# Attention and a gated layer on one core: output weights beside the gated values, maxima moved by ScalarE, earlier token sums, other ranks

## The chip, the cores and the metric

The kernel runs on one core of a Trainium2 chip. The core has TensorE (PE in the profile, with its weight loads as PEld), VectorE (DVE), ScalarE (ACT), GpSimd (POOL) and SyncE (SP); SP issues every transfer of this kernel. The metric is the device time of one execution in microseconds.

## The reference

Linear attention over 8 batches of 8 heads with 576 tokens and 64 columns, and a gated layer on its output, all in float32:

```python
def phi(x):
    proj = np.einsum('bhsd,df->bhsf', x, w_phi)
    proj = proj - np.max(np.abs(proj), axis=-1, keepdims=True)
    return np.concatenate([np.exp(proj), np.exp(-proj)], axis=-1)
q_p, k_p = (phi(q), phi(k))
kv = np.einsum('bhsf,bhsd->bhfd', k_p, v)
z = np.sum(k_p, axis=2)
num = np.einsum('bhsf,bhfd->bhsd', q_p, kv)
den = np.einsum('bhsf,bhf->bhs', q_p, z)[..., None] + 1e-06
x = (num / den).transpose(0, 2, 1, 3).reshape(4608, 512)
gate = 1.0 / (1.0 + np.exp(-(x @ w_gate)))      # w_gate: 512 x 1536
return (gate * (x @ w_val) @ w_out)             # w_out: 1536 x 512
```

## The kernel before

**Arithmetic.** Every large product is made of three: each operand is split into a high part, rounded to the float32r format, and a low part, the rest, and high x high, high x low and low x high are summed in PSUM. So each weight and each activation lies in SBUF twice (`wh`/`wl`, `xh`/`xl`, `hh`/`hl`).

**Stages.** The 1536 hidden columns are twelve blocks `j` of 128.
- *Attention*: 32 pairs of heads (`attend(i)`, four to a batch). For each, PE projects K token by token (L431, tails L447/L451) and Q feature by feature (L536; the first three pairs, `on_pe`, do Q another way, L497 to L518). DVE takes K's maxima (L437) and subtracts them (L466), ACT makes the two exponentials (L478). Then PE multiplies with V (L620) and sums K's features over the tokens (L634), turns the result (L646), and forms the numerators (L662) and denominators (L680).
- *First blocks*: blocks 0 to 3 for nine chunks `c` of 512 tokens (`gate`, L913, and `mm_out`, L970), woven between the pairs. A chunk needs all the pairs of its tokens; chunks 7 and 8 need the last batch. Results go to DRAM (`yscr`).
- *Passes*: blocks 4 to 11, four at a time (`pass_over`, two halves of six stretches of 768 tokens). There the gate and value products are done with seven instead of eight block products (`group`, L1228) from combined weights (`combine`), and the output products are L1310. One stretch is 168 matmuls of L1228 and 72 of L1310.

**Q's maxima** (pairs from the fourth on). DVE takes maxima within squares of 32 by 32 (L558) into `pm`, 128 partitions by 36. `across` (L567 to L576), one operation of the plan on DVE, takes the maximum over all 128 partitions: two copies of 64 partitions and four of 32 into `pn`, and two maxima. Then come the transposition to `mb` (L579) and the subtraction (L586).

**Token sums.** For pairs `i < ONPE` PE does the sums over K's tokens in five steps of four matmuls, four with `ones` as weights and one with `halves`: 20 in the source, 40 in the profile, where each of these float32 matmuls stands twice. For `i >= ONPE` DVE adds four blocks of tokens first (L599, L606, into `su`), and L634 has two steps, 16 matmuls in the profile.

**SBUF.** `low` (86 KiB a partition) and `flat` last through the kernel. Attention's buffers lie at the other end, and are replaced at `swap()`, once all attention work is done, by `high` (72 KiB) and `more`. In `low`, in the first part: `r_wh`, `r_wl` 0 to 32 KiB, `r_xh`, `r_xl` to 48, `r_oh`, `r_ol` to 64, `r_hh`, `r_hl` to 84. For the passes the same memory is cut anew: `r_X` (the tokens) 0 to 42 KiB, `r_y1` to 48, `r_h` (the gated values) to 72, `r_stage` to 86. `high` holds `r_G`, the combined weights, 0 to 56 KiB and `r_wo`, the output weights of four blocks, to 72; for chunk 7 its tokens `r_x7` lie at 42 to 58 KiB. In L1310 the gated values are the stationary operand and `wo` the moving one; in L1228 the weights from `high` are stationary and the tokens from `low` moving; in L913 and L970 weights `wh`/`wl` and gated values `hh`/`hl` are stationary, tokens and output weights `r_oh`/`r_ol` moving.

**Output weights.** For the first half, `out_weight` computes the weights of blocks 4 to 7 straight into `r_wo`. Those of blocks 8 to 11 are computed during the first stretches into `r_stage`, stored to DRAM (`kept`, `wscr`) and fetched into `r_wo` for the second half (`fetched`).

**Order.** `Plan` is a list scheduler that runs when the kernel is built. Each operation has an engine, an estimated time, its buffers and a rank; of the operations of an engine that could start at about the same time, the lowest rank goes first, and on PE a change of kind adds `STICK` to the rank. The result is a fixed order of instructions on each engine and of transfers in SP's queue. Ranks: pair `i` has `due(i) = START + PERIOD * (i - 4)` from the fifth pair on, its kv step `KOFF` later, its numerators `NOFF` later. A chunk has `due` of the pair after its last one, plus `LEAD`; its block `j` has `2 * j * FSTEP` more, its outputs `(8 + t) * FSTEP`. Weight `m` of block `j` has `(3 * j + m) * WSTEP`. The passes begin at rank `due(32) + 60 + 150`.

Of the kernel before, what the change touches and what calls it, by code (L numbers as in the profile page):

```python
# [20 lines left out]
P = 128  # L21
# [16 lines left out]
CELL = 64  # L38
RA = 86 << 10
RB = 72 << 10  # L40
FB = 15 << 10
NQ = 3
LATE = 7
ONPE = 12
BANKS = 5
PERIOD = 16.4
START = 56.0
LEAD = 90.0
STICK = 6.0
WAT = 0.0  # L50
WSTEP = 6.0
RAW = 6
XN = 4
HN = 5
FSTEP = 4.5
KOFF = 20.0
NOFF = 40.0
HSTEP = 2.0
# [209 lines left out]
def attention_moe(  # L268
# [87 lines left out]
    r_h = x.ring(8, 2 * HT)  # L356
    r_stage = x.ring(2, 7 * 2 * P)
    x = high()
    r_G = x.ring(8, 7 * 2 * P)
    r_wo = x.ring(8, DM)  # L360
    r_x7 = high(42).ring(2 * NC4, CW)
# [45 lines left out]
    def attend(i):  # L407
# [121 lines left out]
        else:  # L529
# [23 lines left out]
            )  # L553
            pm, pn = at("pm", 2, [P, nj]), at("pn", 2, [P, nj])
            mb = at("mb", 1, [P, 2, S])
# [10 lines left out]

            def across():  # L567
                vec.tensor_copy(pn()[0:64], pm()[64:128])
                vec.tensor_copy(pn()[64:128], pm()[0:64])
                vec.tensor_tensor(pm(), pm(), pn(), op=ALU.max)  # L570
                for a in range(4):
                    o = a ^ 1
                    vec.tensor_copy(pn()[a * 32 : a * 32 + 32], pm()[o * 32 : o * 32 + 32])
                vec.tensor_tensor(pm(), pm(), pn(), op=ALU.max)

            plan.op("DVE", 1.6, 0.16, across, [], [pm, pn], r + 7)  # L576
            dve(
# [751 lines left out]
    for n in range(2):  # L1329
        r = base - 30.0 + 30.0 * n  # L1330
        for m in range(2):
            ws[n, m] = combine(n, m, r + 10.0 * m, [r_G], [])
        for j in pair(n):
            wo[j] = out_weight(j, r + 20.0, [r_wo], [])
    start = base + 150.0
    for dc in range(NDC):
        r = start + SPAN * dc
        pass_over(
            (0, 1), dc, r, ws, wo, yscr, ymark, lambda c, t: y2scr[c][t], y2mark
        )  # L1340
        if dc < 4:
            n, m = 2 + dc // 2, dc % 2
            mark = marks[n, m] = Buf()
            kept(combine(n, m, r + KEEP, [r_stage], [done]), gscr[n, m], mark, r + KEEP)
            j = JA + 4 + dc
            mark = marks[j] = Buf()
            kept(out_weight(j, r + KEEP + 10.0, [r_stage], [done]), wscr[j], mark, r + KEEP)

# [68 lines left out]
```

## Time and profile before

| | us |
|---|---|
| median of three runs | 1168.27 |
| lowest, highest | 1164.08, 1170.7 |
| the profiled execution's own time | 1167.91 |
| its span, first to last instruction | 1166.0 |
| last matmul of attention (L680) ends | 516.4 |
| first product of the passes (L1228) | 598.7 |
| one stretch of a pass (L1228, L1310) | 29.13 + 16.79 |
| DVE, ACT busy | 933.6, 583.3 |

How to read it: a line such as `L1310 PE MATMUL gate<-high,low` names the source line, the engine, the operation, the tile that is written and the arenas that are read; `128x512` is partitions by columns. Where a helper records operations, the line is that of the helper. Matmuls are pipelined: the time of one is the distance of the starts, not the length of its bar, so a row of the chain divided by its count gives it.

### The profile page before, as it was taken

To read this page: it belongs to the slowest core of one execution; us is meant where nothing else is said; L and a number is where in the kernel's file an instruction comes from. 1 tells how busy PE (TensorE), PEld (TensorE's weight loads), DVE (VectorE), ACT (ScalarE), POOL (GpSimd) and SP (SyncE) were. 2 spreads that over 40 slices of the span, in tenths; PEclk is the share of its full clock that TensorE was granted. 3 is DMA by queue.
4 is the path that set the end of the run, shared out by engine and by line. 5 is a ranking of instruction groups with operands and counts; after the bars stand their busy time and mean duration, and the time that the engine had idled before them with its cause. 6 is when DMAs were issued, how large, how long until landed. Compare 5 with 4: busy or idle time off the path is not lost.

```text
span 1166.0 us, 22301 instructions
## 1 busy us (share of the span) xinstructions
PE 1148.7 (99%) x8796; PEld 939.5 (81%) x8796; DVE 933.6 (80%) x1793; ACT 583.3 (50%) x1115; POOL 0.7 (0%) x6
## 2 busy tenths in 40 slices
PE   8999999999999999999999999999999999999998
PEld 6666566776676777778879899899899898998997
DVE  6999989888878878848987999998766756857764
ACT  6767776666657666626553444352332332423421
POOL 0000000000000000000000000000000000000000
PEclk9999999999999999999999999999999999999999
DMA  7674553444425353225334646645557424224232
GB/s 235 202 242 126 151 169 120 133 125 126 146 80 160 108 155 103 79 79 193 116 99 152 204 142 238 181 147 179 163 178 278 143 93 122 81 89 157 59 91 82
DMA packets 97136, 166.88 MB, mean 143 GB/s; under 512 B 18568, under 2 KB 43272, under 8 KB 97032
## 3 DMA queue, kind: packets, MB, share of 16 engines
q1 hardware_dynamic: 97032, 165.46, 44.8%
q8 instruction: 69, 1.13, 0.4%
q14 instruction: 35, 0.29, 0.1%
HBM read 117.96 MB, written 47.32 MB: 142 GB/s over the span
## 4 chain that ended last, share of the span: by engine, by line
PE 85%; DVE 8%; DMA 5%; ACT 1%; issue 1%; SPq 0%; DVEq 0%; ACTq 0%
PE bank L1228 30%; PE gate L1310 17%; PE gate L913 11%; PE gate L970 7%; PE bank L620 4%; PE bank L662 3%; PE bank L431 2%; DMA rb<-den 2%; PE bank L680 2%; PE bank L913 2%; PE bank L536 1%; DMA den<-dn 1%; PE bank L970 1%; DVE d L586 1%; PE bank L634 1%; PE bank L646 1%
## 5 line engine op out<-in xcount | busy, mean ns | idle before, releaser
L1228 PE MATMUL bank<-low,high 128*128 128x384 f32 x2016 | 352.3, 336 | 0.9 <-DVE low L1190 0.7
L1228 PEld LDWEIGHTS bank<-low,high 128*128 128x128 f32 x2016 | 349.8, 188 | 2.7 <-DVE low L1190 1.0
L1310 PE MATMUL gate<-high,low 128*128 128x512 f32 x864 | 203.6, 395 | 0.0
L1310 PEld LDWEIGHTS gate<-high,low 128*128 128x128 f32 x864 | 162.3, 188 | 37.9
L913 PE MATMUL gate<-low 128*128 128x512 f32 x708 | 168.4, 394 | 1.2 <-ACT flat L948 0.6
L913 PEld LDWEIGHTS gate<-low 128*128 128x128 f32 x708 | 130.8, 188 | 30.2 <-issue 1.2
L478 ACT ACTIVATE ek<-ek 128x512 f32<-128x512 f32 (+1 forms) x192 | 96.7, 526 | 27.5 <-DVE ek L466 26.2
L1241 DVE TENSOR_TENSOR more<-more,bank 128x384 f32<-128x384 f32 x104 | 57.2, 550 | 43.0 <-PE bank L1228 42.8
L970 PE MATMUL gate<-low 128*128 128x512 f32 x372 | 89.8, 395 | 0.0
L970 PEld LDWEIGHTS gate<-low 128*128 128x128 f32 x372 | 68.6, 188 | 15.0 <-issue 1.0
L620 PE MATMUL bank<-ek,vin 128*32 128x256 f32 x1240 | 73.3, 381 | 4.5 <-ACT d L544 4.1
L1241 DVE TENSOR_TENSOR flat<-flat,bank 128x384 f32<-128x384 f32 x87 | 47.9, 551 | 34.9 <-PE bank L1228 34.2
L620 PEld LDWEIGHTS bank<-ek,vin 128*32 128x32 f32 x1240 | 37.4, 110 | 45.8 <-issue 10.2
L1138 DVE TENSOR_TENSOR flat<-gate,low 128x512 f32<-128x512 f32 x72 | 49.3, 685 | 24.8 <-PE gate L1310 15.0
L437 DVE TENSOR_REDUCE mk<-bank 128x4 f32<-128x512 f32 (+1 forms) x92 | 49.0, 551 | 19.7 <-PE bank L431 17.1
L1186 ACT CAST low<-more 128x768 fp32r<-128x768 f32 x36 | 30.1, 836 | 66.2 <-DVE more L1177 66.2
L466 DVE TENSOR_TENSOR ek<-bank,mk 128x512 f32<-128x512 f32 (+1 forms) x92 | 48.2, 550 | 0.6 <-ACT d L549 0.2
L937 ACT CAST low<-flat 128x512 fp32r<-128x512 f32 x36 | 22.3, 621 | 49.6 <-DVE flat L962 45.4
L589 ACT ACTIVATE eq<-d 128x1152 f32<-128x1152 f32 x29 | 33.9, 1167 | 24.5 <-DVE d L586 24.4
L1283 ACT CAST low<-flat 128x384 fp32r<-128x384 f32 x44 | 22.0, 511 | 45.0 <-DVE flat L1279 44.9
L1266 ACT ACTIVATE more<-more 128x384 f32<-128x384 f32 x37 | 19.4, 525 | 47.6 <-DVE more L1241 47.6
L431 PE MATMUL bank<-wk,kin 64*128 64x128 f32 x496 | 38.5, 289 | 4.5 <-DMA kin<-k 4.4
(187 smaller groups left out, 1701.0 us busy)
## 6 DMA issues: line engine op xcount, KB each, us to landing
flat<-w_moe SPq DMA_DIRECT2D x36, 512.0 KB
low<-xs SPq DMA_DIRECT2D x46, 256.0 KB
kin<-k SPq DMA_DIRECT2D x32, 320.0 KB
qin<-q SPq DMA_DIRECT2D x32, 320.0 KB
vin<-v SPq DMA_DIRECT2D x32, 320.0 KB
ys<-flat SPq DMA_DIRECT2D x36, 256.0 KB
low<-ys SPq DMA_DIRECT2D x36, 256.0 KB
yt<-flat SPq DMA_DIRECT2D x36, 256.0 KB
```

Of the source, the lines that this page charges most:

```text
L431: nc.tensor.matmul(pk[hd]()[:, t, :], x()[head(hd), t * P : t * P + P], wk[head(hd), :], start=True, stop=True,)
L437: vec.tensor_reduce(mx, pk, axis=AX.X, op=ALU.max, apply_absolute_value=True)
L466: vec.tensor_tensor(ek[g]()[:, :, F:], src, mk[g]()[:, :ns].unsqueeze(2).broadcast_to([P, ns, F]), op=ALU.subtract,)
L478: lambda g=g, sg=sg: act.activation(ek[g]()[:, :, sg * F : sg * F + F], ek[g]()[:, :, F:], AF.Exp, scale=1.0 - 2.0 * sg,),
L620: nc.tensor.matmul(o_[o : o + Q, : 2 * F], vx()[:, 2 * t + hd, o % D : o % D + Q], (e0, e1)[hd][:, t, :] if t < 4 else e2[:, 0, :], start= ...
L662: nc.tensor.matmul(nm()[o : o + Q, :], w()[:, sg, o : o + Q], es[sg]()[:, o // D, cs], start=sg == 0, stop=sg == 1, tile_position=(0, o),)
L913: nc.tensor.matmul(o(), a()[:, ws], x(), start=cc + n == 0, stop=cc == NC4 - 1 and n == 2,)
L970: nc.tensor.matmul(acc(), a()[:, ts], w(), start=first and i == 0, stop=last and i == 2)
L1138: lambda: vec.tensor_tensor(y(), acc(), y1().bitcast(F32), op=ALU.add),
L1228: nc.tensor.matmul(o()[:, :HT], s()[:, ws], y()[:, cc, :], start=first and cc + i_ == 0, stop=cc + i_ == 3, skip_group_check=not first,)
L1241: lambda: vec.tensor_tensor(o(), p(), q()[:, :HT], op=ALU.add),
L1310: nc.tensor.matmul(acc(), s()[:, h, o : o + P], w(), start=i + e + k_ == 0, stop=i + e + k_ == 4,)
```

## The change

- `r_wo` moves from `high` to the end of `low` (72 to 88 KiB), and `r_stage` from there to `high` behind `r_G`; `low` grows by 2 KiB and `high` shrinks by 2. A ring `r_swo` of seven slots lies over `r_stage`, in which output weights are staged.
- The output weights of blocks 4 to 7 too are computed in `r_swo`, stored and fetched into `r_wo`, once the first blocks' work is done (`done`). Those of blocks 8 to 11 use `r_swo` in place of `r_stage`.
- `across` is cut up: its six copies are operations of ACT (`moved`), in two groups, and its two maxima (`larger`) operations of DVE between them. `pm` and `pn` have one buffer instead of two.
- `ONPE` goes from 12 to 8.
- The constants of the ranks are set anew.

```diff
-RA = 86 << 10
-RB = 72 << 10
+RA = 88 << 10
+RB = 70 << 10
-ONPE = 12
+ONPE = 8
-PERIOD = 16.4
-START = 56.0
-LEAD = 90.0
-STICK = 6.0
+PERIOD = 18.4
+START = 50.0
+LEAD = 60.0
+STICK = 8.0
-WSTEP = 6.0
+WSTEP = 8.0
-FSTEP = 4.5
-KOFF = 20.0
-NOFF = 40.0
+FSTEP = 6.2
+KOFF = 18.4
+NOFF = 36.0
...
-    r_stage = x.ring(2, 7 * 2 * P)
+    r_wo = x.ring(8, DM)
     x = high()
     r_G = x.ring(8, 7 * 2 * P)
-    r_wo = x.ring(8, DM)
+    r_stage = x.ring(2, 7 * 2 * P)
+    r_swo = high(56).ring(7, DM)
...
-            pm, pn = at("pm", 2, [P, nj]), at("pn", 2, [P, nj])
+            pm, pn = at("pm", 1, [P, nj]), at("pn", 1, [P, nj])
...
-            def across():
-                vec.tensor_copy(pn()[0:64], pm()[64:128])
-                vec.tensor_copy(pn()[64:128], pm()[0:64])
+            def moved(step):
+                for o in range(0, P, step):
+                    a = o ^ step
+                    act.copy(pn()[o : o + step], pm()[a : a + step])
+
+            def larger():
                 vec.tensor_tensor(pm(), pm(), pn(), op=ALU.max)
-                for a in range(4):
-                    o = a ^ 1
-                    vec.tensor_copy(pn()[a * 32 : a * 32 + 32], pm()[o * 32 : o * 32 + 32])
-                vec.tensor_tensor(pm(), pm(), pn(), op=ALU.max)
-
-            plan.op("DVE", 1.6, 0.16, across, [], [pm, pn], r + 7)
+
+            for n_, step in enumerate((64, 32)):
+                plan.op(
+                    "ACT", 0.13 * P / step, 0.17, lambda step=step: moved(step),
+                    [pm], [pn], r + 7 + n_ / 2,
+                )
+                plan.op("DVE", 0.11, 0.16, larger, [pn], [pm], r + 7.2 + n_ / 2)
...
         for j in pair(n):
-            wo[j] = out_weight(j, r + 20.0, [r_wo], [])
+            mark = marks[j] = Buf()
+            kept(out_weight(j, r + 20.0, [r_swo], []), wscr[j], mark, r + 20.0)
     start = base + 150.0
+    for j in (*pair(0), *pair(1)):
+        wo[j] = fetched([r_wo], DM, wscr[j], marks[j], start - 20.0, [done])
...
-            kept(out_weight(j, r + KEEP + 10.0, [r_stage], [done]), wscr[j], mark, r + KEEP)
+            kept(out_weight(j, r + KEEP + 10.0, [r_swo], [done]), wscr[j], mark, r + KEEP)
```

## What the change does to the time: a prediction

> **What bounds the kernel now.** I read the page's engines and slices first, then the stretches of 25 us over the start, then the chain that ended last, and then single lines and tiles.
>
> ```profile
> PE 1148.7 (99%) x8796; PEld 939.5 (81%) x8796; DVE 933.6 (80%) x1793; ACT 583.3 (50%) x1115; POOL 0.7 (0%) x6
> PEclk9999999999999999999999999999999999999999
> PE 85%; DVE 8%; DMA 5%; ACT 1%; issue 1%; SPq 0%; DVEq 0%; ACTq 0%
> ```
>
> TensorE (PE) is busy for 1148.7 of 1166.0 us at an undiminished clock, and 85% of the chain is its own work. So a change can win in two ways only: PE's work gets shorter, or the few holes in it close. The stretches show where the holes are:
>
> ```profile
> 0.00:25.00 25.00, 20.64 (x242) 16.59 (x246) 16.48 (x38) 14.68 (x31) 0.70 (x6) 1.00 0.76 253
> 75.00:100.00 25.00, 23.74 (x212) 17.22 (x211) 24.81 (x48) 15.54 (x29) 0.00 (x0) 1.00 0.34 102
> 125.00:150.00 25.00, 22.36 (x346) 14.38 (x338) 22.66 (x54) 18.17 (x36) 0.00 (x0) 1.00 0.54 161
> 150.00:175.00 25.00, 23.90 (x363) 14.88 (x354) 21.17 (x46) 19.48 (x41) 0.00 (x0) 1.00 0.57 174
> sum 250.00, PE 237.30 PEld 162.50 DVE 221.08 ACT 174.91 POOL 0.70; mean PE 23.73 PEld 16.25 DVE 22.11 ACT 17.49 POOL 0.07
> ```
>
> (Columns: stretch, its length, then busy us of PE, weight loads, DVE, ACT, POOL; clock; DMA share; GB/s.) In the first 250 us PE idles 12.7 us, 4.4 of them in the first 25; behind 25 us it is 8.3. There DVE is the fuller engine (24.81 of 25 at 75 to 100 us). PE's remaining idle time is about 5 us, mostly the tail behind the last product. The chain gives the price of each kind of product:
>
> ```profile
> 147.27 1.09 PE bank L634 x40
> ...
> 506.88 5.49 PE gate L913 x24
> 512.37 2.08 PE bank L662 x32
> 514.45 1.94 PE bank L680 x32
> 516.39 16.54 PE gate L913 x72
> 532.93 5.60 PE bank L913 x24
> 538.53 10.90 PE gate L970 x48
> 549.43 8.40 PE bank L913 x36
> 557.83 8.40 PE gate L913 x36
> 566.23 2.74 PE bank L913 x12
> 568.97 10.88 PE bank L970 x48
> ...
> 602.45 8.20 PE gate L970 x36
> 610.65 2.72 PE bank L970 x12
> 613.37 27.04 PE bank L1228 x156
> 640.41 16.79 PE gate L1310 x72
> 657.21 29.13 PE bank L1228 x168
> ```
>
> From 613 us on the chain is only L1228 and L1310 in turns, twelve rounds of 29.13 + 16.79 us with nothing between.
>
> **The change, part by part.**
>
> *Output weights into `low`.* All of L913, L970 and L1310 multiply 128x128 weights with 512 columns, yet they don't cost the same. L970 at 568.97 takes 10.88/48 = 226.7 ns each; both its operands lie in `low`. L913 at 549.43 and 557.83 takes 8.40/36 = 233.3 ns; this is chunk 7, whose moving operand is `r_x7` in `high`, its stationary one in `low`. L1310 takes 16.79/72 = 233.2 ns; its moving operand `wo` is in `high`, its stationary one, the gated values, in `low`. L1228 turns this round: stationary `high`, moving `low`, 29.13/168 = 173.4 ns for 384 columns. If it shares L970's fixed part, a column costs (226.7 - 173.4)/128 = 0.416 ns and that part is 13.6 ns; for L1310 and chunk 7 it would be 20. So, by these rows, the dear case is a moving operand in `high`, and the change takes it away: 72 x 6.5 ns = 0.47 us a round, **-5.6 us** in twelve. Ends: -5.6, and 0 if the new place at 72 to 88 KiB of `low` is dear as well (rows cover moving operands of `low` only up to some 66 KiB).
>
> The Trainium skill speaks against this term: "TensorE: Matmul & The Clock Gate", section "Back-to-back issue gap", makes the gap a function of the column count and the clock alone, about 216 ns at 512 columns, and "SBUF — State Buffer", section "Who interferes with whom", has TensorE wait for nobody at its two read ports. By them this term would be 0. The trace does not agree, with two gaps (226.7 and 233.2) at one count, neither of them 216.
>
> What it costs: the first half's four output weights are now stored and fetched again. The eight fetches cannot land before chunk 8's last output product has left `r_hh`/`r_hl`, at 613.37, and are needed at 640.41: 27 us of cover.
>
> ```profile
> DMA packets 5720, 11.68 MB, mean 234 GB/s; under 512 B 528, under 2 KB 2576, under 8 KB 5717
> 890.28 1.82 SPq L1117 DMA_DIRECT2D high<-wo  x4
> 893.15 2.17 SPq L1117 DMA_DIRECT2D high<-wo  x4
> 616.16 16.99 SPq L790 DMA_DIRECT2D flat<-w_moe  x3
> ```
>
> The same eight fetches are issued within some 5 us at 890, and 2.1 MB at that stretch's mean of 234 GB/s are 9 us. So 0. If they fell behind the weight loads that hold SP's queue from 616.16 to 633.15, they would land near 633 + 4 + 9 = 646 and PE would stand 5.5 us, once. Their rank (start - 20) lies before these loads' (start + 30). The eight stores wait in SP's queue for DVE's last step of each weight; behind them are the x loads of the first pass, which have the same 27 us.
>
> *Token sums from the ninth pair.* Each kv step costs less PE:
>
> ```profile
> 265.43 0.40 PE L634 MATMUL bank<-su,ones 128*32 128x128 f32 x8
> 265.65 0.40 PE L634 MATMUL bank<-ek,halves 128*32 128x128 f32 x8
> 265.87 0.67 PE L662 MATMUL bank<-eq,kv 128*32 128x288 f32 x8
> ```
>
> From 265.43 to 265.87 are 0.44 us, against 1.09 for 40 matmuls. Four pairs more: 4 x 0.65 = **-2.6 us**.
>
> *DVE and ACT around it.*
>
> ```profile
> L573 DVE COPY pn<-pm x116: 170/174/180, 43.1 to 489.3; 32x36 f32<-32x36 f32 x116
> L568 DVE COPY pn<-pm x29: 177/178/180, 42.5 to 488.1; 64x36 f32<-64x36 f32 x29
> L569 DVE COPY pn<-pm x29: 175/176/179, 42.7 to 488.3; 64x36 f32<-64x36 f32 x29
> L599 DVE TENSOR_TENSOR s<-ek x40: 629/649/686, 170.5 to 493.4; 128x512 f32<-128x512 f32 x40
> L606 DVE TENSOR_TENSOR su<-s x40: 361/398/422, 176.4 to 494.6; 128x256 f32<-128x256 f32 x40
> L549 ACT COPY d<-bank 128x128 f32<-128x128 f32 x29 | 7.7, 264 | 0.2
> ```
>
> Off DVE go 4 x 174 + 178 + 176 ns = 1.05 us in 29 pairs; onto it come 2 x 649 + 2 x 398 = 2.1 us in four pairs. The early stretch, where DVE is the fuller engine, holds pairs 4 to 11: 8 x 1.05 = 8.4 off, 4 x 2.1 = 8.4 on, so 0. ACT gets six copies of 36 columns, each below the 264 ns of 128 columns, under 1.6 us a pair; it is busy 50%. But DVE now waits twice a pair for ACT, and behind a waiting maximum stand, in DVE's order, the products' own steps and the next K maxima. If these waits ate the whole saving, 8.4 us of DVE work would be left over in that stretch. Ends: 0 and +8.4; I take 0, since the plan can put other work between. From pair 12 on PE has no hole for it to cause or cure. One buffer for `pm` and `pn` costs nothing: DVE runs the pairs' steps in order.
>
> *Ranks.* They decide who goes first, twice with a price. (a) Early. Chunk 0's rank falls from 146 to 110 and chunk 1's from 211.6 to 183.6, while a batch of pairs spreads over 73.6 instead of 65.6; the weights come at 8 instead of 6. So product work lasts longer into the stretch at 125 to 175 us, where PE idles 3.7 us for lack of it, above all here:
>
> ```profile
> 144.91 2.37 PE L620 MATMUL bank<-ek,vin 128*32 128x256 f32 x40 [2.64 <-ACT d L544]
> ```
>
> Ends 0 and -8.3; I take this one wait, **-2.6**. (b) Where attention ends. Chunks 7 and 8 need the last pair. Its last matmuls end at 516.39 and chunk 7's first product is at 532.93: 16.5 us, covered now by three weight blocks of chunk 6 (16.54 us), with its outputs (10.9) in reserve. Before, chunk 6's blocks have ranks 539.6, 548.6, 557.6, 566.6 and the last pair's numerators 538.8; after, 551.6, 564.0, 576.4, 588.8 against 582.8. So three blocks go ahead, perhaps half of the fourth too, as one block slipped in at 506.88 while the pair's copies were under way. Left are half a block and the outputs, 2.7 + 10.9 = 13.6 of 16.5 us: **+2.9**. Ends: 0, and +16.5 if the outputs go ahead too. The weights' combination begins when attention is done, too:
>
> ```profile
> L1093 DVE TENSOR_TENSOR high<-flat,high x16: 411/417/419, 534.9 to 610.4; 128x256 fp32r<-128x256 f32 x16
> ```
>
> Its last step starts at 610.4; the first pass needs it in the fourth quarter of its 29.13 us before 640.41, from 633 on. With 20 us in hand it stays at 0 for a shift of 16.
>
> **Sum**, against the profiled execution's own 1167.91 us (span 1166.0 and 1.9 around it; the median of the three runs is 1168.27, 0.4 above): -5.6 - 2.6 - 2.6 + 2.9 = -7.9, so **1160.0 us**.
>
> **Rivals.**
> - *The place of the moving operand is not the cause.* Then L1310 stays at 16.79 and the rest holds: 1165.6. For it: no row has a moving operand in `low` at 72 KiB or above, so a bound between 66 and 72 would do it. Against: chunk 7 and L1310 share nothing but that operand's home. The Trainium skill's two sections named above stand for this case as well.
> - *The cover at attention's end goes.* If chunk 6's outputs too run before the last pair, PE stands 16.5 us at about 525 instead of 2.9: 1160.0 + 13.6 = 1173.6, slower than before; it is slower than the median of before from the point at which the cover falls below 5.3 us (16.5 less the 2.9 and 8.3 lost). For it: product work moves ahead by some 20 in rank and blocks slip in at 506.88. Against: the outputs' ranks begin at 601.2, behind 582.8.
> - *DVE becomes the early bound.* The new waits eat the saving: up to +8.4 and no early gain; with half of it, 1160.0 + 2.6 + 4.2 = 1166.8.
> - *The early holes close altogether:* -8.3 instead of -2.6, 1154.3.
>
> **How the numbers follow.** Forecast 1160.0 (own range 1156.5 to 1163): 0.48. Early holes closed: 0.14. Other cause of the 6.5 ns: 0.14. DVE bound early: 0.12. Cover gone: 0.12. A measurement of this kernel can tell about 0.5%, 5.8 us, from no change. Faster than 1162.4: 0.44 of the forecast, the 0.14 and 0.03 of the DVE case: 0.61. Slower than 1174.1: 0.07 of the cover case and 0.01 of the DVE case: 0.08. Within: 0.31. The range of 8 in 10 leaves out most of the cover case above and the far end of the closed holes below: 1152 to 1168.
>
> **What would show it.** L1310 x72 at 16.3 instead of 16.79 with a source in `low` proves the first term, 16.79 with that source refutes it. L634 with 16 matmuls from pair 8 on, 0.44 us, the second. In the stretches, PE idle from 25 to 250 us under 8.3 shows (a); a wait of chunk 7's first L913 after the last L680 shows (b). DVE maxima on `pm` with idle time released by ACT before 175 us would speak for the DVE rival. I am wrong above all if the ranks move more than I can read off them: I weighed two places and every queue's order is set anew.

## The result, and the profile after

| | before | after |
|---|---|---|
| median us | 1167.71 (8 runs, 1164.08 to 1170.7) | 1162.29 (8 runs, 1160.49 to 1164.99) |
| ratio | | 0.9950, 95% interval 0.9937 to 0.9963 |
| the profiled execution's own time, span | 1167.91, 1166.0 | 1162.59, 1160.8 |

The changed kernel is 5.4 us faster by the medians, 5.3 by the profiled executions. Line numbers move: up to the copies of Q's maxima by 1, behind them by 5 (L1310 is L1315, L1228 is L1233, L913 is L918, L970 is L975, L620 is L625, L634 is L639). The engines of the page, after:

```profile
PE 1143.2 (98%) x8700; PEld 938.1 (81%) x8700; DVE 912.0 (79%) x1635; ACT 620.2 (53%) x1289; POOL 0.7 (0%) x6
```

TensorE has 96 matmuls less and 5.5 us less of busy time, VectorE 21.6 us less, and ScalarE 36.9 more. The chain after, where the passes begin (start, us, what):

```profile
601.90 8.20 PE gate L975 x36
610.10 2.72 PE bank L975 x12
612.82 27.04 PE bank L1233 x156
639.86 16.36 PE gate L1315 x72
656.22 5.20 PE bank L1233 x30
661.45 24.42 PE bank L1233 x138
685.87 4.34 PE gate L1315 x19
```

The output products of one stretch take 16.36 us in place of 16.79, and the passes begin at 612.8 us as before (613.4). So nearly all that is won in the end is won in the passes: from their begin to the end of the span 552.6 us before, 548.0 after. What was won in the first 600 us was lost again there. The stretches of the start, after (same columns as in the prediction):

```profile
75.00:100.00 25.00, 24.28 (x245) 15.25 (x245) 24.40 (x49) 21.80 (x44) 0.00 (x0) 1.00 0.51 165
100.00:125.00 25.00, 21.94 (x309) 14.16 (x306) 22.33 (x39) 22.87 (x58) 0.00 (x0) 1.00 0.50 144
125.00:150.00 25.00, 24.16 (x273) 15.56 (x274) 20.16 (x38) 17.36 (x38) 0.00 (x0) 0.93 0.48 155
150.00:175.00 25.00, 25.00 (x233) 18.11 (x235) 19.30 (x35) 18.07 (x44) 0.00 (x0) 1.00 0.44 137
...
sum 250.00, PE 239.31 PEld 166.50 DVE 206.72 ACT 185.34 POOL 0.70; mean PE 23.93 PEld 16.65 DVE 20.67 ACT 18.53 POOL 0.07
```

The holes of TensorE at 125 to 175 us are smaller (0.8 us idle in place of 3.7), but a new one of 3.1 us stands at 100 to 125, where ScalarE is now the fullest engine beside TensorE (22.87 of 25). In all, TensorE idles 10.7 us in the first 250 against 12.7. The new hole ends with this wait of TensorE, for a copy (L545) that stands in ScalarE's order behind the moved copies of Q's maxima (L571); the last four of these take 0.91 us:

```profile
123.08 0.45 ACT L571 COPY pn<-pm 64x36 f32<-64x36 f32 x2
124.27 0.91 ACT L571 COPY pn<-pm 32x36 f32<-32x36 f32 x4
125.21 1.07 ACT L545 COPY d<-bank 128x512 f32<-128x512 f32 x2
125.84 1.19 PE L667 MATMUL bank<-eq,kv 128*32 128x288 f32 x8 [2.45 <-ACT d L545]
...
129.34 0.66 PE L685 MATMUL bank<-eq,kv 128*32 128x288 f32 x8
```

Behind the hole the clock granted to TensorE was half for 3.4 us, which the 0.93 in the row of 125 to 150 us comes from:

```profile
125.60:129.00 3.40, 3.15 (x28) 1.38 (x32) 3.40 (x5) 1.08 (x3) 0.00 (x0) 0.51 0.57 196
```

From start to start the eight matmuls at 125.84 took 0.97 us, the eight of the same form at 129.34 took 0.48. By such steps I estimate that the half clock cost 1.6 us. It is counted as busy time in the stretches. The waits of TensorE between 500 and 615 us, after (us in total, times, longest):

```profile
PE bank L918 <- ACT high L897: 1.2, 1, 1.2
PE bank L1233 <- DVE low L1195: 1.1, 1, 1.1
PE bank L918 <- DVE high L902: 0.7, 2, 0.4
```

The first products of chunk 7 (L918) wait for its tokens, which ScalarE and VectorE write into `high`. No such wait stood in the profile of before. The wait of L1233 has a counterpart there: the first twelve products of the passes took 3.43 us here and 3.56 before.

For the comparisons below I use one table. The lost time of TensorE is the sum, over all its matmuls, of the distance from a start to the next, less the pace of the same kind where nothing disturbs it (226.7 ns for 512 columns in L913, L970 and L1310, 173.4 ns for L1228, and for attention the time of an undisturbed block, such as 0.99 us for 16 matmuls of L431, divided by its count). It holds waits, changes of kind, slow operands and stretches at a lower clock. The undisturbed sum is 1121.4 us with twelve pairs of token sums on TensorE and 1118.8 with eight; with some 8.4 us ahead of the first matmul and behind the last start, the rows add up to the spans.

| kernel | median us | ratio, 95% interval | span | lost to 250 | 250 to 500 | 500 to 615 | behind 615 |
|---|---|---|---|---|---|---|---|
| before | 1167.7 | | 1166.0 | 22.3 | 5.7 | 2.6 | 5.6 |
| after | 1162.3 | 0.9937 to 0.9963 | 1160.8 | 20.6 | 6.0 | 6.1 | 1.0 |
| e1: weights moved alone | 1159.3 | 0.9905 to 0.9932 | 1157.4 | 20.2 | 5.5 | 1.0 | 1.0 |
| e2: sums alone | 1168.9 | 0.9992 to 1.0015 | 1165.7 | 23.6 | 6.6 | 2.6 | 5.7 |
| e3: copies alone | 1173.3 | 1.0020 to 1.0043 | 1171.7 | 26.7 | 6.8 | 2.6 | 5.8 |
| e4: ranks alone | 1173.8 | 1.0029 to 1.0054 | 1172.5 | 19.7 | 10.6 | 7.0 | 5.6 |
| e6: after, copies back on VectorE | 1171.3 | 1.0011 to 1.0040 | 1168.2 | 21.8 | 10.8 | 6.2 | 2.2 |
| e7: after, old ranks | 1165.4 | 0.9957 to 0.9986 | 1165.0 | 26.5 | 8.3 | 1.1 | 2.1 |
| e8: after, sums for 12 pairs | 1164.4 | 0.9942 to 0.9974 | 1162.7 | 19.3 | 5.8 | 6.9 | 1.0 |
| e10: before, `high` pushed down | 1164.1 | 0.9938 to 0.9970 | 1163.5 | 22.6 | 5.8 | 2.2 | 3.0 |
| e11: e1, `high` pushed down | 1161.1 | 0.9933 to 0.9961 | 1157.7 | 20.9 | 5.3 | 0.5 | 1.2 |
| e12: after, chunk 6 later, `high` pushed down | 1161.1 | 0.9922 to 0.9951 | 1160.0 | 20.5 | 6.5 | 2.9 | 3.0 |

Each ratio is against runs of the kernel before on the same chip, whose medians were between 1167.7 and 1169.2; it is an estimate of its own and can differ by 0.001 from the quotient of two medians. The span and the lost times are those of one execution each, and not always a middle one: e10's and e7's are the slowest of their five and eleven, e11's the fastest of its five. The clock differs, too. Ahead of the last microseconds it was half for 3.4 us in the profiles of after (from 125.6 us), e12 (from 126.2) and e6 (from 548.9), and for 6.8 us in e3 (from 73.3) and e7 (from 72.3). By the steps of the matmuls there I estimate 1.6 us of lost time each for the first three and some 2 for e3 and e7. In e3 and e7 it is no single execution's matter: the mean granted clock is 0.995 to 0.997 in all of theirs, against 0.998 to 1.000 in those of e1. Each of these stretches stands at a wait of TensorE, but its length alone does not tell: the 2.64 us at 144.91 in the kernel before were followed by a full clock.

### The profile page after: what moved, and what is told of

Same layout as the page of the kernel before. It is cut to its first block, busy times and chain, and to the rows that moved or that the text cites. A ratio compares the mean times of both kernels' runs of the same rounds, so it can differ in the third digit from the quotient of the medians.

```text
span 1160.8 us, 22170 instructions
## 1 busy us (share of the span) xinstructions
PE 1143.2 (98%) x8700; PEld 938.1 (81%) x8700; DVE 912.0 (79%) x1635; ACT 620.2 (53%) x1289; POOL 0.7 (0%) x6
## 4 chain that ended last, share of the span: by engine, by line
PE 76%; DVE 8%; DMA 8%; ACT 5%; issue 2%; SPq 1%; DVEq 0%; ACTq 0%
PE bank L1233 30%; PE gate L1315 17%; PE gate L918 9%; PE gate L975 5%; PE bank L667 4%; PE bank L625 3%; DMA rb<-den 3%; DMA den<-dn 2%; PE bank L432 2%; PE bank L685 2%; DMA low<-xs 1%; PE bank L537 1%; ACT ek L479 1%; DVE d L591 1%; DVE mb L584 1%
## 5 line engine op out<-in xcount | busy, mean ns | idle before, releaser
L1233 PE MATMUL bank<-low,high 128*128 128x384 f32 x2016 | 352.9, 336 | 1.1 <-DVE low L1195 1.1
L1233 PEld LDWEIGHTS bank<-low,high 128*128 128x128 f32 x2016 | 349.8, 188 | 3.2 <-DVE low L1195 1.4
L1315 PE MATMUL gate<-low 128*128 128x512 f32 x864 | 198.8, 390 | 0.0
L1315 PEld LDWEIGHTS gate<-low 128*128 128x128 f32 x864 | 162.0, 188 | 33.1
L918 PE MATMUL gate<-low 128*128 128x512 f32 x696 | 167.9, 395 | 1.3 <-DVE low L765 1.0
L918 PEld LDWEIGHTS gate<-low 128*128 128x128 f32 x696 | 128.1, 188 | 30.3 <-issue 3.0
L479 ACT ACTIVATE ek<-ek 128x512 f32<-128x512 f32 (+1 forms) x192 | 93.1, 527 | 16.7 <-DVE ek L467 15.7
L975 PE MATMUL gate<-low 128*128 128x512 f32 x384 | 92.6, 394 | 0.0
L1246 DVE TENSOR_TENSOR more<-more,bank 128x384 f32<-128x384 f32 x99 | 54.5, 551 | 39.0 <-PE bank L1233 37.1
L975 PEld LDWEIGHTS gate<-low 128*128 128x128 f32 x384 | 70.7, 188 | 14.6 <-DVE mb L707 0.5
L625 PE MATMUL bank<-ek,vin 128*32 128x256 f32 x1200 | 70.3, 379 | 0.0
L1143 DVE TENSOR_TENSOR flat<-gate,low 128x512 f32<-128x512 f32 x72 | 49.3, 686 | 26.5 <-DMA out<-flat 12.3
L1246 DVE TENSOR_TENSOR flat<-flat,bank 128x384 f32<-128x384 f32 x82 | 45.2, 551 | 29.1 <-PE bank L1233 28.7
L625 PEld LDWEIGHTS bank<-ek,vin 128*32 128x32 f32 x1200 | 38.5, 110 | 28.0 <-ACT pn L571 0.7
L571 ACT COPY pn<-pm 64x36 f32<-64x36 f32 (+1 forms) x174 | 38.2, 219 | 22.9 <-DVE pm L574 19.0
L1288 ACT CAST low<-more 128x384 fp32r<-128x384 f32 x51 | 25.5, 514 | 46.5 <-DVE more L1284 46.5
L667 PE MATMUL bank<-eq,kv 128*32 128x288 f32 x472 | 41.3, 421 | 3.2 <-ACT d L545 2.4
```

The costliest lines, as they stand in the source:

```text
L479: lambda g=g, sg=sg: act.activation(ek[g]()[:, :, sg * F : sg * F + F], ek[g]()[:, :, F:], AF.Exp, scale=1.0 - 2.0 * sg,),
L571: act.copy(pn()[o : o + step], pm()[a : a + step])
L625: nc.tensor.matmul(o_[o : o + Q, : 2 * F], vx()[:, 2 * t + hd, o % D : o % D + Q], (e0, e1)[hd][:, t, :] if t < 4 else e2[:, 0, :], start= ...
L667: nc.tensor.matmul(nm()[o : o + Q, :], w()[:, sg, o : o + Q], es[sg]()[:, o // D, cs], start=sg == 0, stop=sg == 1, tile_position=(0, o),)
L918: nc.tensor.matmul(o(), a()[:, ws], x(), start=cc + n == 0, stop=cc == NC4 - 1 and n == 2,)
L975: nc.tensor.matmul(acc(), a()[:, ts], w(), start=first and i == 0, stop=last and i == 2)
```

## The experiments

### The four parts, one at a time

**e1, the output weights alone.** The kernel before with the new places of `r_wo`, `r_stage` and `r_swo`, the detour through DRAM, and one buffer for `pm` and `pn` (the memory is needed):

```diff
-RA = 86 << 10
-RB = 72 << 10
+RA = 88 << 10
+RB = 70 << 10
...
-            wo[j] = out_weight(j, r + 20.0, [r_wo], [])
+            kept(out_weight(j, r + 20.0, [r_swo], []), wscr[j], mark, r + 20.0)
...
```

> The kernel before with the output weights alone moved beside the gated values (stored and fetched once more for the first half; one buffer each for the two small tiles of maxima, so that it fits). If the place of the moving operand sets the price of an output product, a stretch of 72 goes from 16.79 to about 16.36 us and the whole by 12 x 0.43 = -5.2 us, with at most 0.5 us back where the fetch falls in the first stretch. If the gain of the whole change came from ranks or sums and the products' pace from their surroundings, 16.79 stays and the time is that of before, within 1 us.

It took 1159.28 us, 0.9918 of before: 9.9 us less, twice what the passes account for, and more than the whole change. The output products and chunk 7's products, by line, tile and form (last the ns of one, lowest, median and highest, then first and last start):

```profile
L1311 PE MATMUL gate<-low x864: 387/389/402, 636.2 to 1153.3; 128*128 128x512 f32 x173
```

```profile
L914 PE MATMUL bank<-high,low x60: 394/394/394, 530.2 to 554.9; 128*128 128x512 f32 x60
```

In the kernel before the output products are these:

```profile
L1310 PE MATMUL gate<-high,low x864: 388/395/398, 640.2 to 1161.9; 128*128 128x512 f32 x173
```

A bar is longer than the distance to the next one, since matmuls are pipelined, but 395 against 389 ns is the same step as 233.3 against 226.7 in the distances. So moving the weights removes the dear case in L1310, and chunk 7, whose tokens stay in `high`, keeps it. The table tells where the 8.6 us of the spans came from: 4.6 in the passes, 1.6 at the handover (the first pass begins with 6 products ahead of chunk 8's outputs where before it had 12, which took 3.56 us in place of 2.08 because they waited for their inputs), and 2.1 in the first 250 us. There the orders of TensorE, VectorE and ScalarE are those of before, and 1.0 of the 2.1 lies in the first 25 us. The same products, in the kernel before and in e1:

```profile
8.14 0.82 PE bank L497
...
8.03 0.42 PE bank L498
```

TensorE begins at half its pace in both, and the trace has the full clock from 7.9 us on in e1, from 10.3 in the kernel before. e11, with the same orders as e1, has it from 10.1 on, so that microsecond belongs to the execution and not to the edit.

**e2, the token sums alone.** The kernel before with one constant:

```diff
-ONPE = 12
+ONPE = 8
```

> The kernel before with the token sums on VectorE from the ninth pair, and nothing else. If TensorE is the bound there, four kv steps are 0.65 us shorter: -2.6 us. If VectorE is the bound early, as a rival has it, its 2.1 us more in each of four pairs stay: between 0 and +8.4 us.

The ratio is 1.0003 (0.9992 to 1.0015): the 2.6 us that TensorE saves come back as 2.3 of lost time. Two stretches of this kernel:

```profile
150.00:175.00 25.00, 21.20 (x270) 12.40 (x259) 23.16 (x46) 17.43 (x35) 0.00 (x0) 1.00 0.66 182
175.00:200.00 25.00, 23.97 (x229) 15.86 (x231) 24.57 (x56) 16.95 (x32) 0.00 (x0) 1.00 0.38 115
```

VectorE is at 24.57 of 25 us in the second, and TensorE idles 3.8 us in the first, where it idled 1.1 before. Its longest wait there, 1.3 us, is for a copy (L669) that stands in ScalarE's order behind an exponential, and that one had waited for VectorE's subtraction:

```profile
ACT eq L589 <- DVE d L586: 1.0, 1, 1.0
```

So VectorE had no room there for the sums.

**e3, the copies alone.** The kernel before with the new `moved` and `larger`, and two buffers each for `pm` and `pn`:

```diff
-            plan.op("DVE", 1.6, 0.16, across, [], [pm, pn], r + 7)
+            for n_, step in enumerate((64, 32)):
+                plan.op("ACT", 0.13 * P / step, 0.17, lambda step=step: moved(step), [pm], [pn], r + 7 + n_ / 2)
+                plan.op("DVE", 0.11, 0.16, larger, [pn], [pm], r + 7.2 + n_ / 2)
```

> The kernel before with the six copies of the maxima on ScalarE, and nothing else. If VectorE's early hours set the time, its 1.05 us less in each of some eight pairs give up to -8 us. If the two new waits of VectorE and ScalarE's 1.3 us more in each pair weigh there instead, it is slower, by up to 5 us. I expect them to cancel: within 1.5 us of before.

It is slower, by 4.2 us (1.0020 to 1.0043), and loses them in the first 250 us. The longest wait of TensorE between 50 and 125 us:

```profile
PE gate L917 <- ACT low L761: 4.9, 1, 4.9
```

The products of the first chunk (L917 here) stand 4.9 us for the high parts of their tokens, which ScalarE makes (L761). ScalarE itself was idle just before; it got the tokens from VectorE (L755), late, as the chain over that place shows (start, us, what):

```profile
71.86 0.69 DVE low L870
72.55 0.67 DVE xp L755
73.22 0.60 DVE flat L826
```

and VectorE is the full engine there:

```profile
50.00:75.00 25.00, 19.84 (x269) 13.50 (x261) 24.03 (x41) 17.36 (x38) 0.00 (x0) 0.97 0.88 267
```

So it is not ScalarE's extra work (six copies of 0.22 us a pair) that TensorE waits for in this place. The copies' new place gives all engines another order, and in this one the first chunk is begun before VectorE, with 24.0 of 25 us taken, has its tokens ready. The wait cost more than its 4.9 us, since the clock was half around its end and behind it:

```profile
75.80:80.10 4.30, 4.30 (x10) 3.44 (x11) 3.78 (x7) 1.83 (x3) 0.00 (x0) 0.50 0.67 241
```

The matmuls of 512 columns stood 427 ns apart here.

**e4, the ranks alone.** The kernel before with the eight new constants (`PERIOD`, `START`, `LEAD`, `STICK`, `WSTEP`, `FSTEP`, `KOFF`, `NOFF` and no other change; `ONPE` stays at 12).

> The kernel before with the new constants of the ranks alone. By the trace of the changed kernel the handover from attention to chunk 7 costs 3.5 us of TensorE and the early holes give 1.7 back: +1.9 us, that is slower by 1 to 3 us. If the ranks were what pays, it is 3 us or more faster.

It is 4.6 us slower (1.0029 to 1.0054). The first 250 us gain 2.6 us, as the prediction had it, but the steady stretch loses 4.9 and the handover 4.4. The waits between 500 and 615 us show the same handover as in the changed kernel:

```profile
PE bank L1228 <- DVE low L1190: 1.5, 1, 1.5
PE bank L913 <- ACT high L892: 1.5, 1, 1.5
PE bank L913 <- DVE high L897: 0.5, 2, 0.3
```

The four alone add up to -9.9 + 0 + 4.2 + 4.6 = -1.1 us, the change gives -5.4. So they depend on one another, and the next three runs each take one part out of the changed kernel.

### One part taken out

**e6, the copies back on VectorE.** The changed kernel with `across` as it was:

```diff
-            for n_, step in enumerate((64, 32)):
...
+            plan.op("DVE", 1.6, 0.16, across, [], [pm, pn], r + 7)
```

> The changed kernel with the copies of Q's maxima back on VectorE, all else as changed. If the parts add up: the copies alone cost 4.2 us on the kernel before, so 1162.3 - 4.2 = 1158. If they work together (the sums on VectorE need the room that the copies leave there): the hole of 5.3 us at 100 to 125 us shrinks to some 2, but VectorE fills at 150 to 200 us as with the sums alone, where 9.3 us went lost against 1.1 in the changed kernel: 1162.3 - 3.3 + 8.2 = 1167, with 1163 if the new ranks spread the sums better.

1171.3 us, 9.0 more than the changed kernel: adding up is refuted, and the hole that I expected at 150 to 200 us isn't where it is lost either. 4.8 of the 7.4 us between the spans lie in the steady stretch, 250 to 500 us, though the profile shows no wait of TensorE there. Groups of this kernel in that stretch (busy us, mean ns):

```profile
L971 PE MATMUL gate<-low 128*128 128x512 f32 x192 | 48.2, 399 | 0.0
...
L537 PE MATMUL bank<-qin,wk 64*128 64x512 f32 x56 | 16.5, 608 | 0.0
```

The same two in the changed kernel, where the first is L975:

```profile
L975 PE MATMUL gate<-low 128*128 128x512 f32 x192 | 46.7, 395 | 0.0
...
L537 PE MATMUL bank<-qin,wk 64*128 64x512 f32 x56 | 14.4, 590 | 0.0
```

The same matmuls take 1.5 and 2.1 us more. In e4 and here the products of the first blocks stand in 34 pieces among attention's matmuls in this stretch, in the changed kernel in 27: the planner, with one long step of 1.6 us on VectorE and the new ranks, cuts product work into blocks of 12 instead of 24 matmuls to fill in, and each cut costs at both its edges. That these edges make up the 4.8 us is my reading, no run changes them alone. So the new ranks are bad with the copies on VectorE (e4, e6: 10.6 and 10.8 us lost from 250 to 500) and not with them on ScalarE (6.0 and 5.8).

**e7, the old ranks.** The changed kernel with the eight rank constants of before.

> The changed kernel with the rank constants of the kernel before. If the parts add up: the constants alone cost 4.6 us, so 1162.3 - 4.6 = 1157.7, with the handover at 500 to 615 us back from 6.1 us lost to 1 (as with the output weights moved alone) and the passes as in the changed kernel. If the new constants are what lets the copies and the sums pass: the early part to 250 us loses 26 us or more as with the copies alone, against 20.6, and the handover's 5 us are gained back: 1162.3 + 6 - 5 = 1163.

1165.4 us, 3.1 more than the changed kernel, so adding up is refuted here too; it is more even than the second expectation. The early part loses 26.5 us as the copies alone did, and by the same wait and half clock, in the list of TensorE's waits from 50 to 125 us:

```profile
PE gate L918 <- ACT low L762: 4.4, 1, 4.4
```

The handover is back at 1.1. So, by these two profiles, the new ranks are worth 5.9 us early, if the copies are on ScalarE, and 2.3 in the steady stretch, and they cost 5.0 at the handover.

**e8, the sums for twelve pairs on TensorE.** The changed kernel with `ONPE = 12`.

> The changed kernel with K's token sums on TensorE for twelve pairs again. If the sums' place is worth what TensorE saves: four pairs by 0.65 us, 1162.3 + 2.6 = 1164.9. If it is given back on VectorE as it was when done alone: 1162.3, the hole at 100 to 125 us being smaller by what TensorE does longer there.

1164.4 us, 2.1 more, near what the first expectation said, but this doesn't decide between the two. The intervals of the two ratios overlap (0.9942 to 0.9974 and 0.9937 to 0.9963), and the nine executions fall into two groups: four from 1160.8 to 1161.8 us and five from 1164.4 to 1164.8. The median is the lowest of the upper group, the profile is of that group too, and the lower one is as fast as the changed kernel. So what the sums are worth in the changed kernel, between nothing and the 2.6 us that TensorE saves, is not shown. The profile has this stretch at 100 to 125 us:

```profile
100.00:125.00 25.00, 23.91 (x333) 15.20 (x329) 22.42 (x42) 23.41 (x58) 0.00 (x0) 1.00 0.50 146
```

TensorE idles 1.1 us here, against 3.1 with the sums on VectorE, and no half clock follows. In these two profiles this part of the saving is given back.

### What makes 512 columns cost 233 ns

**e5, places.** Twelve tiles, every pair of them as stationary and moving operand:

```python
for i, w in enumerate(tiles):
    for j, m in enumerate(tiles):
        for k in range(24):
            matmul(bank, w[:, (k % 8) * 128 : ...], m[:, 2048 + 512 * (k % 2) : ...])
```

> A measurement by itself, none of the reference is computed: twelve tiles of 16 KiB each side by side in SBUF (sa lowest, from 16 KiB, to sl, ending at 208 KiB), and for every pair (i, j) 24 matmuls 128x128 by 128x512 with the stationary in tile i and the moving in tile j. Before's slow matmuls took 233.3 ns with the moving at 177 KiB and above and the stationary at 50 to 122 KiB, its fast ones 226.7 ns with the moving between 50 and 138 KiB. If the address of the moving operand decides: every row reads 226.7 for j up to some tile between sh and sk and 233.3 from there on, whatever i is. If the distance of the moving above the stationary decides: slow in a triangle, j above i by 3 tiles or more, and the column of sl fast for the stationary in sl itself. If it was something of the kernel around them (transfers writing into the same tiles, other engines reading them): all 144 groups within 0.5 ns of one another.

All 144 groups took the same, 226.7 ns from start to start, but for the very first, where eight of the first nine matmuls took some 427 ns each, as under the half clock of e3. The ends of the field, lowest and highest tile, by form:

```profile
L36 PE MATMUL bank<-sl,sa 128*128 128x512 f32 x24 | 5.6, 389 | 0.0
...
L38 PE MATMUL bank<-sa,sl 128*128 128x512 f32 x24 | 5.6, 389 | 0.0
...
L40 PE MATMUL bank<-sl 128*128 128x512 f32 x24 | 5.6, 389 | 0.0
```

So neither the address nor the distance of the two operands decides. What the tiles of this run have in common is their offset: each begins 128 bytes behind a multiple of 2048. In the kernel before, as it is built, `low` begins at byte 51232 of a partition, 32 behind a multiple of 2048, and `high` at 140256, which is 992 behind one. The moving operands of L1310 and of chunk 7 lie in steps of 2048 from there.

**e9, offsets.** The same matmuls, with tiles whose offset is chosen: 24 for the moving operand, four for the stationary one (wa 0, wb 32, wc 96, wd 992).

> A measurement by itself, none of the reference is computed: one core of matmuls 128x128 by 128x512 with nothing beside them, for 24 offsets of the moving operand (its address in SBUF modulo 2048 bytes, tiles ma to mx: 0, 16, 32, 48, 64, 80, 96, 112, 128, 160, 192, 224, 256, 288, 352, 480, 512, 544, 736, 992, 1024, 1056, 1504, 2016) and four of the stationary (wa to wd: 0, 32, 96, 992), 24 matmuls each. In the kernel before, the slow movings lie at 992 modulo 2048 and the fast ones at 32; in the twelve tiles of the measurement before this one all lay at 128. If the offset decides: some of the offsets read 226.7 ns and mt (992) 233.3, and the others say by which power of two. If it is the offset against that of the stationary: the slow ones move from wa to wd. If neither: all 96 groups at 226.7, and it is what the other engines do beside them.

The moving operand at 992, with each of the four stationary ones:

```profile
L43 PE MATMUL bank<-mt,wa x24: 395/396/396, 118.3 to 123.6; 128*128 128x512 f32 x24
L43 PE MATMUL bank<-mt,wb x24: 394/394/394, 251.6 to 257.0; 128*128 128x512 f32 x24
L43 PE MATMUL bank<-mt,wc x24: 390/394/404, 385.4 to 390.7; 128*128 128x512 f32 x24
L43 PE MATMUL bank<-mt,wd x24: 389/389/389, 518.8 to 524.1; 128*128 128x512 f32 x24
```

The second row is chunk 7's case, stationary at 32 and moving at 992, and it has chunk 7's 394 ns to the digit. The fourth row has both at 992 and is fast. Nothing else runs beside them. From start to start (mean ns of matmuls 3 to 23 of each 24), for some of the offsets of the moving operand:

| stationary at | 16 | 32 | 80 | 96 | 224 | 256 | 288 | 352 | 480 | 512 | 992 | 1056 |
|---|---|---|---|---|---|---|---|---|---|---|---|---|
| 0 | 231.5 | 233.3 | 231.1 | 233.7 | 232.9 | 226.7 | 233.5 | 233.3 | 232.9 | 226.7 | 233.4 | 233.5 |
| 32 | 226.7 | 227.7 | 233.4 | 229.4 | 233.2 | 233.1 | 227.2 | 229.0 | 233.4 | 232.9 | 233.3 | 227.2 |
| 96 | 233.3 | 233.5 | 226.7 | 227.7 | 233.6 | 234.0 | 233.3 | 227.2 | 233.5 | 234.0 | 232.4 | 233.4 |
| 992 | 230.0 | 229.5 | 231.1 | 232.4 | 227.2 | 233.4 | 228.9 | 232.4 | 228.2 | 233.5 | 226.7 | 228.9 |

The fast cells are those in which both operands have the same offset modulo 256 bytes (992 is 224 modulo 256; 32 goes with 32, 288 and 1056): 226.7 to 228.2 ns in all 15 of these but the run's first group, which began at the slow pace of e5's. Of the other 80, 69 took 231 to 235 ns, nine took 229 to 230, and two neighbours (16 with 32, 80 with 96) 226.7. Why these are fast too, the run doesn't tell.

**e10, the offset alone.** One number of the kernel before; `more`, which lies above `high`, grows into memory that was unused, and `high` begins at 139296, 32 behind a multiple of 2048. All engines' orders and all transfers are those of before.

```diff
-FB = 15 << 10
+FB = (15 << 10) + 960
```

> The kernel before with one number changed: 960 bytes more in the arena above, which push the arena with the output weights and chunk 7's halves down from 992 modulo 2048 to 32, with every engine's order as before. If the offset decides: L1310 x72 takes 16.36 us in place of 16.79 and chunk 7's first L913 x84 about 0.6 us less, 1168.9 - 5.2 - 0.6 = 1163. If what decides is that the output weights lie in another arena than the gated values, or what is written there beside the matmuls: L1310 stays at 16.79 and the time at 1168.9, ratio 1.000.

1164.06 us, 0.9954 (0.9938 to 0.9970). The output products, still with a source in `high`:

```profile
L1310 PE MATMUL gate<-high,low x864: 387/389/501, 640.4 to 1159.5; 128*128 128x512 f32 x173
```

389 ns in place of 395 without moving anything to `low`, and 16.36 us a stretch (the chain's row at 640.58). The median gained 4.4 us of the expected 5.8. The profiled execution, the slowest of the five, gained less, and its chain shows one reason: in the third stretch the tokens came late (start, us, what),

```profile
725.67 7.82 DMA low<-xs
```

and TensorE lost 2.0 us at 736 to 742, the longest gaps in L1310 being 0.5 us behind ScalarE and 0.5 behind VectorE. Whether the faster passes are to blame isn't shown: e1 and e11, with passes as fast, lose 1.0 and 1.2 us behind 615 us, against 3.0 here.

**e11, the move and the offset.** e1 with the same 960 bytes.

> The kernel before with the output weights moved (as in the first run) and the upper arena pushed down by 960 bytes as well, so that chunk 7's halves lie at 32 modulo 2048 too. If the offset decides: chunk 7's matmuls with these halves (L914 here, 233 ns each) go to 227 ns, 96 x 6.6 = 0.6 us, 1159.3 - 0.6 = 1158.7. The move alone lost 20.2 us before 250 us where the kernel before lost 22.3 with the same orders there; if that belongs to the move, it stays near 20; if it was one execution's luck, it is at 22 and the time at 1160.5.

1161.07 us, 0.9947 (0.9933 to 0.9961), where e1 had 0.9918 (0.9905 to 0.9932). Chunk 7's products are fast now, with their moving operand still in `high`:

```profile
L914 PE MATMUL bank<-high,low x60: 389/389/389, 530.9 to 555.2; 128*128 128x512 f32 x60
```

That is 0.5 us, and 500 to 615 us lose 0.5 in place of 1.0. The time doesn't show it: the two spans, 1157.4 and 1157.7, are as good as equal, and the medians lie 1.8 the other way. Whether the 1159.3 of e1 was luck of those runs or the chip, these two medians don't tell; the version without the copies, sums and ranks takes 1159 to 1161, no more than the changed kernel and perhaps a little less. The first 250 us lose 20.9 here, 1.4 less than before, though the full clock came as late as there (10.1 us); I can't settle why. One buffer less for `pm` and `pn` moves attention's tiles by 64 bytes modulo 256 as well, but 40 matmuls of its largest group (L620 before) take 2.30 us in both kernels' chains.

### The handover

**e12, chunk 6 held back.** The changed kernel with chunk 6's rank 14 later, and `high` pushed down:

```diff
-FB = 15 << 10
+FB = (15 << 10) + 960
...
+                if c == LATE - 1:
+                    r += 14.0
```

> The changed kernel with chunk 6 held back by 14 in rank and the upper arena pushed down by 960 bytes. If the handover's loss is chunk 7 coming too early for its maxima, because too little of chunk 6 is left when attention ends at 529 us: the 6.1 us lost between 500 and 615 us fall to 2 and chunk 7's 96 matmuls gain 0.6, 1162.3 - 4.1 - 0.6 = 1157.6. If the chain behind attention is what ends last however much TensorE has left: the loss stays at 5 to 6 and the time at 1161.5.

The loss at the handover falls from 6.1 to 2.9 us, 0.6 of it by chunk 7's faster matmuls, and the two waits that are left there are none of chunk 7's:

```profile
PE gate L975 <- ACT low L942: 0.6, 1, 0.6
PE gate L975 <- DVE low L944: 0.4, 1, 0.4
```

So it was the cover that was missing. The span gains 0.8 only: the passes begin at 608.9 instead of 612.8, by the chains, but 1.0 of that is that six of their products in place of twelve stand ahead of chunk 8's outputs, and they lose 2.0 us more in their first stretches, for the most part waiting for VectorE to empty a bank. In the waits behind 615 us:

```profile
PE bank L1235 <- DVE more L1248: 1.2, 3, 0.8
```

So the loss went as the first expectation said, and the time came out as the second did: 1161.06, 1.2 below the changed kernel, with overlapping intervals.

## Why the prediction was right, and where it wasn't

The forecast of 1160.0 stood for the profiled execution's conditions; that of the changed kernel took 1162.59. The sum was -7.9 us and the spans give -5.2.

- **Output weights, -5.6.** The passes became 4.6 us shorter. The rows were read rightly: 16.36 us a stretch (16.3 was said), 12 x 0.43 = 5.2, and 0.5 lost once in a stretch of L1233, which took 29.65 us (656.22 to 685.87) in place of 29.13. The fetches cost nothing, as said: no idle time stands before L1315. The cause that the prediction gave is wrong, though. "The dear case is a moving operand in `high`" falls with e5, e10 and e11: the same operand in the same arena is fast once its offset agrees with that of the stationary one. That the term came out all the same is luck: the move brought the operands to one offset along with the new place. The sign that the prediction named, 16.3 us with a source in `low`, could not tell the two apart. The argument had two arenas and two paces, and every slow row had its operand in `high`; but an arena differs from another in more than its place, and the offset was one of the things. The rival that the place is not the cause was true in its words and wrong in its time, for the same reason.
- The Trainium skill's "TensorE: Matmul & The Clock Gate", section "Back-to-back issue gap", would have made this term 0. It does not hold here: e9 has 226.7 to 234.7 ns at one count of columns behind its first group.
- **Token sums, -2.6.** TensorE's undisturbed work shrank by just that. What became of it was not said: alone it is worth 0.0 us (e2), and in the changed kernel e8 leaves it open.
- **VectorE and ScalarE, 0.** The prediction set 8.4 us of work off VectorE against 8.4 onto it in the early pairs, and took no loss from the new waits. In the changed kernel that came near; with the old ranks it did not: 4.2 us alone (e3), and 5.9 us early in e7 against the changed kernel. That is near the rival in which VectorE is the early bound (half of its 8.4 us), which so came true for a kernel with other ranks. The sign for it, VectorE's maxima waiting for ScalarE, was there and small in the changed kernel: 1.3 us in five waits up to 175 us. The price of the copies shows elsewhere, in ScalarE's order at 124 us. How much of the loss in e3 and e7 is the copies themselves and how much the order of the work, no run separates.
- **Ranks, early, -2.6.** The lost time fell by 1.7. The wait of 2.64 us at 144.91 is gone; the new hole at 100 to 125 us, released by ScalarE, took part of it back, and some 1.6 us of half clock behind it, which the prediction had no term for, is in the 1.7.
- **Ranks, handover, +2.9.** It was +3.5, but not by the sum that was made. All four blocks of chunk 6 went ahead, where three and a half were said, so only the outputs (10.9 us) were left. From attention's end at 529.06 to chunk 7's first product at 541.47 it took 12.4 us, not 16.5: the 16.5 was the length of the cover in the kernel before, where chunk 7 had not waited. So the first wait was 1.5 us, and 1.8 more were lost among the next 60 products, whose tokens came one after another; the prediction had one wait. That the two errors nearly cancel is luck. e12 confirms that the cover decides, and e4 that it comes from the ranks.

The mis-sized terms add up to the 2.7 us but for rounding: passes 1.0, early holes 0.9, handover 0.6, and 0.3 lost in the steady stretch, which the prediction had at 0. All four went the same way, against the change.

What the prediction lacks is that terms of different parts were added as if each could be had without the others. Three of the four parts alone are worth nothing or cost 4 to 5 us. Together they come to nearly nothing as well: in the spans -2.6, -1.7, +3.5 and +0.3 us, that is -0.5 of the 5.2. e11, which has none of the three, takes 1161.1 against the changed kernel's 1162.3, and e1 1159.3. Nearly all that the change gains, it gains through one offset.

## What to carry to other kernels

When two groups of equal matmuls differ by a few ns each, compare the byte offsets of their operands before their places: here one number that pads an arena was worth 4.4 us of 1168, with no instruction moved. Ranks, copies and sums that shift work between engines are one change, not three; test them both alone and by taking each out of the whole, since the first told the opposite of the second for two of three, the copies and the ranks. Work that is moved ahead can be missing later, here as cover at the handover. Look at the granted clock behind a long wait before you price the wait by its length, and look at all executions before you trust the stages of one profile.

## What the runs showed of the hardware

- A float32r matmul of 128x128 by 128x512 in a steady row takes 226.7 to 228.2 ns where its two operands have the same offset modulo 256 bytes in SBUF, and mostly 231 to 235 ns where they don't (e9, full clock); at one offset, the address, the distance and the tile made no difference (e5, 143 pairs at 226.7 ns behind the first).
- At 384 columns no such difference showed: in e10 the offset of the stationary operand of L1228 went from 224 to 32 modulo 256, that of the moving one being 32, and a stretch took 29.14 us against 29.13.
- Behind some waits of TensorE the granted clock was half for 3.4 us (after, e6, e12) or 6.8 us (e3, e7), and the matmuls of 512 columns took 427 ns there in place of 227. The kernel before waited 2.64 us at 144.91 and had a full clock behind it, the changed kernel waited 2.45 us at 125.84 and had half a clock; what decides, these runs don't show.
- A ScalarE copy of 36 columns from SBUF to SBUF took 219 ns for 32 partitions and for 64 alike:

```profile
L571 ACT COPY pn<-pm x174: 217/219/223, 44.7 to 508.7; 32x36 f32<-32x36 f32 x116, 64x36 f32<-64x36 f32 x58
```

  On VectorE, in the kernel before, the same copies took 174 to 178 ns. So 1.05 us a pair left VectorE and 1.3 us came to ScalarE.
